# VectorE's order in the attention front written by hand, gate products in one bank, one unit of w_in per step

## The chip, the cores and the metric

The kernel runs on one core of a Trainium2 chip. The metric is the time of one execution in microseconds, as the median of several runs; less is better. The engines are TensorE (PE, with its weight loads PEld), VectorE (DVE), ScalarE (ACT), GpSimd (POOL) and SyncE (SP), which issues the DMAs. Each engine works through its own instructions in order and waits on semaphores for the others.

## What is computed

Three layers follow each other, all in float32 (the 18 blocks of 128 tokens are B x S = 2304 rows):

```
# 1 attention, 8 heads of 64, 576 positions, window of 128 back, ALiBi bias
scores = q @ k.T / 8 + slope * -(i - j)          where 0 <= i - j < 128, else -1e9
x = softmax(scores) @ v                          # -> [2304, 512]
# 2 dense layer
h = x @ w_in                                     # 512 -> 2048
g = max(0.01 * h, h)
y = g @ w_out                                    # 2048 -> 512
# 3 experts: 8 of them, 288 tokens each
logits = y @ w_gate                              # assigned greedily, highest logit first
out[mask_e] = relu(y[mask_e] @ w1[e]) @ w2[e]
```

The logits are not taken from y: the kernel multiplies w_out with w_gate first (below: the gate) and then uses g @ (w_out @ w_gate).

## The kernel before, in words

A matmul whose result has to be good to float32 is done as three passes of a faster type: each operand is split into a high part (`wh`, `xh`) and a low part (`wl`, `xl`, value minus high part). w_in and w_out arrive as 64-bit floats; 16 **units** of 128 x 1024 numbers (8 of w_in, 8 of w_out) have to be **converted** on the chip.

The front of the kernel, up to some 440 us of it, is one loop over **steps** s. One step handles one block of 64 queries of the attention, and beside it other work:

- `scores(j)`: 8 products into two PSUM banks of tag "s" (PE); `softmax_exp`: 4 fused add-and-minimum instructions on DVE (L437, into `neg` and `nm`) and 4 exponentials on ACT (L440, with the sums in `sm`); `softmax_norm`: DVE adds and inverts the sums (L447, L448) and scales two of four heads (L453), ACT the other two (L451).
- `transpose_p(j)`: probabilities transposed by PE into two banks of tag "t" and copied by ACT (`pts`, L465); `weighted(j)`: product with v into `xv` (tag "v", one bank); every second block it is split into `xh` (ACT, L490) and `xl` (DVE, L491).
- A unit k at the steps of `CONV_AT`: `conv_abs` (ACT, L345), `conv_high` (three DVE instructions, L356 to L358), `conv_low` (two on DVE, L365 and L366, and one addition on POOL, L368, into `dt`); for w_in also `in_high` (ACT, L350) and `in_low` (L372, on DVE for units 0 and 1, else on POOL). Units 8 to 15 (w_out) are stored to DRAM again.
- The **gate**: for each unit of w_out and each of its two halves h, `gate_transpose` (4 transposes, tag "t", ACT copy `wt`), one step later `gate_product` (4 products into `pg`, tag "l", which has one bank; DVE copy `gs`, L397), one step later `gate_fold` (1 product into `pw`, the same one bank; DVE copy to `wg`, L403).
- 72 **items** (c, fp), 2 (from step 14 on; before that up to 4) in each step as soon as their x and w_in are there: `expand` (24 matmuls into a bank of tag "h", which has two) and `expand_out`: `th` on ACT (L514), `gb` on DVE (L518), store to DRAM.
- From step 31 on the **late** logits: g of the first 6 chunks is loaded back (`gr`, L554) and multiplied with `wg`.

Behind the front follow, one after the other, the product with w_out (`po`, L223) with the assignment of tokens beside it, and the experts (L984, L1003).

What sets the order: for PE and ACT the order in the program text (`ENG_A`); for DVE, POOL and SP a list scheduler of the framework. A tile of a pool with n buffers is written again only when the work on its n-th predecessor is done; so with the one bank of tag "l" each `pg` and `pw` waits for DVE's copy of the one before.

Of the kernel before, what the change touches and what calls it, by code (L numbers as in the profile page):

```python
# [19 lines left out]
P = 128  # L20
# [50 lines left out]
NORM_A = (2, 3)  # L71
STAGES = 2
WINDOW = 128
# [53 lines left out]
def tile_attn_moe_moe2(ctx: ExitStack, tc: tile.TileContext, q_in, k_in, v, w_in, w_out, w_gate, w1, w2, consts, out):  # L127
# [18 lines left out]
    def C(name):  # L146
        return cst[:, COLS[name][0]:COLS[name][1]]
# [155 lines left out]
    with ExitStack() as actx:  # L303
# [70 lines left out]

        gate = {}

        def gate_transpose(k, h):
            w = conv[k]
            if h == 0:
                nc.sync.dma_start(wo_dram[k - 8], w)  # L380
            else:
                conv.pop(k)
            pt = bank("t", f"wtp_{k}_{h}").rearrange("p (d f) -> p d f", d=4)
            for d in range(4):
                T.transpose(pt[:, d, :], w[:, h * DM + d * P:h * DM + d * P + P], ident)  # L385
            wt = cv.tile([P, 4, P], F32, tag="wt", name=f"wt_{k}_{h}")
            A.activation(wt, pt, AF.Copy)
            gate[k, h] = wt

        def gate_product(k, h):  # L390
            wt = gate[k, h]
            pg = bank("l", f"pg_{k}_{h}", bufs=1)[:, :P]
            for d in range(4):
                T.matmul(pg[32 * d:32 * d + 32, :], gsb[:, d, :], wt[:, d, :], start=True,
                         stop=True, tile_position=(0, 32 * d))
            gs = cv.tile([P, P], F32, tag="gs", name=f"gs_{k}_{h}")
            V.tensor_copy(gs, pg)  # L397
            gate[k, h] = gs

        def gate_fold(k, h):  # L400
            pw = bank("l", f"pw_{k}_{h}", bufs=1)[:, :32]
            T.matmul(pw, gate.pop((k, h)), C("fold"), start=True, stop=True)
            V.tensor_copy(wg[:, 2 * (k - 8) + h, :], pw)  # L403


        st = {}
# [1 line left out]
        def scores(j):  # L408


            b, m = divmod(j, SQ)
            nk = keys_before(j)
            s = [bank("s", f"s_{j}_{a}")[:, :2 * nk].rearrange("p (h k) -> p h k", h=2) for a in range(2)]
            qt, t0 = qring[j // 3 % 2], j % 3 * Q
            for hf in range(2):
                for a in range(2):
                    for x in range(2):
                        c, rows = 2 * hf + x, slice(a * D, a * D + D)
                        T.matmul(s[a][x * Q:x * Q + Q, hf, :], qt[rows, c, t0:t0 + Q],  # L419
                                 ktile[b][rows, c, (m + 1) * Q - nk:(m + 1) * Q], start=True, stop=True,  # L420
                                 tile_position=(a * D, x * Q))
            st[j] = dict(nk=nk, s=s)

        def softmax_begin(j):
            d = st[j]
            d["neg"] = [apool.tile([P, 2, 3 * Q], F32, tag="neg", name=f"neg_{j}_{h}") for h in range(2)]
            d["nm"] = apool.tile([P, 4], F32, tag="nm", name=f"nm_{j}", bufs=2)
            d["sm"] = apool.tile([P, 4], F32, tag="sm", name=f"sm_{j}", bufs=2)
            d["pr"] = apool.tile([P, 4, 3 * Q], F32, tag="pr", name=f"pr_{j}", bufs=PRB)

        def softmax_exp(j, hf):
            d = st[j]
            nk = d["nk"]
            for a in range(2):
                i = 2 * hf + a
                neg = d["neg"][hf][:, a, :nk]
                V.tensor_tensor_reduce(  # L437
                    out=neg, in0=d["s"][a][:, hf, :], in1=bias_sb[:, i, 3 * Q - nk:],
                    scale=-0.125, scalar=3e38, op0=ALU.add, op1=ALU.min, accum_out=d["nm"][:, i:i + 1])
                A.activation(d["pr"][:, i, :nk], neg, AF.Exp, scale=-1.0, bias=d["nm"][:, i:i + 1],  # L440
                             accum_out=d["sm"][:, i:i + 1])

        def softmax_norm(j):
            d = st[j]
# [101 lines left out]

        late = {}

        def late_load(c, hf):
            assert not any(x[0] == c for x in items)  # L550
            for f4 in range(2 * hf, 2 * hf + 2):
# [5 lines left out]
        def late_logits(c, hf):  # L557
            for f4 in range(2 * hf, 2 * hf + 2):
                logits(c, f4, late.pop((c, f4)), "t")


# [4 lines left out]
        def at(s, f, *a):  # L566
            after.setdefault(s, []).append((f, *a))

        conv_at = {s: k for k, s in enumerate(CONV_AT)}
        for k, s in list(enumerate(CONV_AT))[8:]:  # L570
            for h in range(2):

                at(s + GLAG + h, gate_transpose, k, h)
                at(s + GLAG + h + 2, gate_fold, k, h)
                at(s + GLAG + h + 1, gate_product, k, h)
        gate_end = CONV_AT[15] + GLAG + 3
        late0 = gate_end + 2
        for c in range(LG0):
            for hf in range(2):
                at(late0 + 2 * c + hf - 1, late_load, c, hf)  # L580
                at(late0 + 2 * c + hf, late_logits, c, hf)
            at(late0 + 2 * c + 2, logits_fold, c)
        late_end = late0 + 2 * LG0

        if True:
# [19 lines left out]
            def prepare(j):  # L605

                if j and j % 3 == 0:
                    load_qk(j // 3 + 1)
# [19 lines left out]
            staged = []  # L628
            scores(0)
            prepare(0)  # L630
            while s <= max(NQ + 1, late_end) or items or pending or tail:

                now = [x for x in items if max(ready.get(x[0], 1 << 30), in_ready.get(x[1] | 1, 1 << 30)) <= s]
                now = now[:ITEMS_0 if s < ITEMS_S else 2]
# [1 line left out]
                    items.remove(x)  # L636
                k = conv_at.get(s)

                if s < NQ:
                    softmax_begin(s)  # L640
                    softmax_exp(s, 0)
                    softmax_exp(s, 1)
                    if s + 1 < NQ:
                        scores(s + 1)
                        prepare(s + 1)
                if 1 < s <= NQ + 1:
                    weighted(s - 2)
                    if (s - 2) % 4 == 3:
                        ready[(s - 2) // 4] = s + XLAG
                if 0 < s <= NQ:  # L650
                    transpose_p(s - 1)
                if s:
                    load_v(s + 1)
# [9 lines left out]
                for f in after.pop(s, ()):  # L663
                    f[0](*f[1:])
                for n, (c, fp) in enumerate(now):
                    expand(c, fp, 0)
                    expand(c, fp, 1)
# [6 lines left out]
                        convert_low(k)  # L674
                if not now:
                    convert_low(k)
                if s + 1 in conv_at:
                    conv_abs(conv_at[s + 1])
# [427 lines left out]
```

## Time and profile before

| | before |
|---|---|
| median of 3 runs | 944.03 us (942.78 to 944.92) |
| profiled execution: time / span | 939.93 us / 938.1 us |
| PE, PEld busy | 847.3 us (90%), 737.0 us (79%) |
| DVE, ACT, POOL busy | 525.8 us, 383.2 us, 109.0 us |
| chain that ended last: PE / DVE / ACT | 78% / 7% / 7% |
| mean granted TensorE clock | 0.970 |

The span goes from the first to the last instruction of the profiled execution. The busy time of PE is made of pipelined matmuls, so a busy PE is not a PE at its peak; what it can't hide are the stretches in which it waits, and those in which its granted clock is below 1. Where a line of the trace has a bracket, it gives the idle time of the engine ahead of it and what ended it.

### The profile page before, as it was taken

To read this page: it belongs to the slowest core of one execution; us is meant where nothing else is said; L and a number is where in the kernel's file an instruction comes from. 1 tells how busy PE (TensorE), PEld (TensorE's weight loads), DVE (VectorE), ACT (ScalarE), POOL (GpSimd) and SP (SyncE) were. 2 spreads that over 40 slices of the span, in tenths; PEclk is the share of its full clock that TensorE was granted. 3 is DMA by queue.
4 is the path that set the end of the run, shared out by engine and by line. 5 is a ranking of instruction groups with operands and counts; after the bars stand their busy time and mean duration, and the time that the engine had idled before them with its cause. 6 is when DMAs were issued, how large, how long until landed. Compare 5 with 4: busy or idle time off the path is not lost.

```text
span 938.1 us, 18698 instructions
## 1 busy us (share of the span) xinstructions
PE 847.3 (90%) x7590; PEld 737.0 (79%) x7590; DVE 525.8 (56%) x1339; ACT 383.2 (41%) x833; POOL 109.0 (12%) x104
## 2 busy tenths in 40 slices
PE   2787878788889989998999999998999999999996
PEld 2577767777778878787777767775889999999995
DVE  5876667536453443224877877877316545555550
ACT  3874635445445554223212131211215555555551
POOL 1323221112110000000000000000011221122211
PEclk9897989999899999999999999999999999999998
DMA  9774545646332796577342423222336555666640
GB/s 286 229 202 153 177 154 176 192 144 213 100 118 64 218 285 173 157 195 221 112 141 75 137 99 127 90 79 69 100 94 195 181 171 187 218 209 188 187 134 26
DMA packets 103637, 147.19 MB, mean 157 GB/s; under 512 B 6144, under 2 KB 74368, under 8 KB 101504
## 3 DMA queue, kind: packets, MB, share of 16 engines
q1 hardware_dynamic: 100480, 136.56, 47.4%
q0 software_dynamic: 3072, 9.44, 2.9%
q8 instruction: 60, 0.98, 0.4%
q14 instruction: 25, 0.20, 0.1%
HBM read 113.21 MB, written 32.77 MB: 156 GB/s over the span
## 4 chain that ended last, share of the span: by engine, by line
PE 78%; DVE 7%; ACT 7%; issue 5%; DMA 2%; POOL 1%; SPq 0%; POOLq 0%; ACTq 0%
PE po L223 23%; PE h L505 20%; PE m L984 10%; PE y L1003 10%; ACT pr L440 3%; PE cnt L804 3%; PE xv L480 2%; PE s L419 2%; PE pt L463 2%; PE lg L532 2%; DVE dt L358 1%; DVE neg L437 1%; PE wtp L385 1%; ACT dt L345 1%; ACT th L514 1%
## 5 line engine op out<-in xcount | busy, mean ns | idle before, releaser
L518 DVE TENSOR_TENSOR gb<-h,th 128x512 f32<-128x512 f32 x72 | 49.6, 690 | 159.4 <-ACT th L514 148.6
L223 PE MATMUL po<-wh_out,gol 128*128 128x512 f32 x272 | 112.0, 412 | 4.2 <-DVE gol L191 4.1
L223 PE MATMUL po<-wh_out,goh 128*128 128x512 f32 x272 | 110.6, 406 | 0.0
L223 PE MATMUL po<-wl_out,goh 128*128 128x512 f32 x272 | 110.4, 406 | 0.0
L514 ACT ACTIVATE th<-h 128x512 f32<-128x512 f32 x72 | 42.8, 596 | 157.0 <-PE h L505 157.0
L505 PE MATMUL h<-xh,wh_in 128*128 128x256 f32 x576 | 96.6, 292 | 7.7 <-DVE gb L518 7.7
L505 PE MATMUL h<-xh,wl_in 128*128 128x256 f32 x576 | 92.6, 284 | 0.0
L505 PE MATMUL h<-xl,wh_in 128*128 128x256 f32 x576 | 91.9, 283 | 0.0
L505 PEld LDWEIGHTS h<-xh,wh_in 128*128 128x128 f32 x576 | 80.5, 197 | 12.0 <-DVE gb L518 8.1
L160 DVE TENSOR_TENSOR wl_w<-st_w,wh_w 128x1024 fp32r<-128x1024 f32 x60 | 72.9, 1225 | 26.7 <-ACT wh_w L159 26.7
L183 ACT ACTIVATE goh<-gin 128x1024 fp32r<-128x1024 f32 x34 | 36.0, 1060 | 126.0 <-DMA gin<-g_dram 107.0
L505 PEld LDWEIGHTS h<-xh,wl_in 128*128 128x128 f32 x576 | 79.7, 195 | 0.2 <-POOL wl_in L372 0.2
L505 PEld LDWEIGHTS h<-xl,wh_in 128*128 128x128 f32 x576 | 79.4, 195 | 0.0
L1003 PE MATMUL y<-hh,wh_w 128*128 128x288 f32 x256 | 77.4, 302 | 0.0
L1003 PE MATMUL y<-hh,wl_w 128*128 128x288 f32 x256 | 75.6, 295 | 0.0
L1003 PE MATMUL y<-hl,wh_w 128*128 128x288 f32 x256 | 75.5, 295 | 0.0
L419 PE MATMUL s<-k,q 64*64 64x192 f32 (+2 forms) x576 | 36.3, 355 | 32.5 <-DVE nm L437 22.3
L159 ACT ACTIVATE wh_w<-st_w 128x1024 fp32r<-128x1024 f32 x60 | 62.4, 1053 | 2.8 <-DMA st_w<-in_w_dram 2.8
L223 PEld LDWEIGHTS po<-wh_out,gol 128*128 128x128 f32 x272 | 51.5, 189 | 15.1 <-DVE gol L191 5.4
L368 POOL TENSOR_TENSOR dt<-dt,de 128x1024 f32<-128x1024 f32 x16 | 38.3, 2392 | 206.7 <-DVE pr L453 79.1
L440 ACT ACTIVATE pr<-neg,nm 128x192 f32<-128x192 f32 (+2 forms) x144 | 60.8, 427 | 0.0
L223 PEld LDWEIGHTS po<-wl_out,goh 128*128 128x128 f32 x272 | 51.4, 189 | 10.2 <-issue 0.2
(220 smaller groups left out, 1607.7 us busy)
## 6 DMA issues: line engine op xcount, KB each, us to landing
st_w<-in_w_dram SPq DMA_DIRECT2D x64, 512.0 KB, 4.0
g_dram<-gb SPq DMA_DIRECT2D x72, 256.0 KB, 3.7
gin<-g_dram SPq DMA_DIRECT2D x34, 512.0 KB, 3.9
gr<-g_dram SPq DMA_DIRECT2D x48, 256.0 KB, 5.4
v<-in_v_dram SPq DMA_DIRECT2D x28, 384.0 KB, 4.7
raw<-in_w_in_dram SPq DMA_DIRECT2D x8, 1024.0 KB, 5.3
raw<-in_w_out_dram SPq DMA_DIRECT2D x8, 1024.0 KB, 5.1
x_dram<-xo SPq DMA_DIRECT2D x17, 256.0 KB, 2.0
```

The costliest lines, as they stand in the source:

```text
L159: A.activation(wh, st, AF.Copy)
L160: lo_engine.tensor_tensor(out=wl, in0=st, in1=wh.bitcast(F32), op=ALU.subtract)
L183: A.activation(wh, st, AF.Copy)
L223: T.matmul(po, g, w, start=(k == 0), stop=(k == 47))
L368: (V if k in ADD_V else GP).tensor_tensor(out=t, in0=t, in1=e, op=ALU.add)
L419: T.matmul(s[a][x * Q:x * Q + Q, hf, :], qt[rows, c, t0:t0 + Q], ktile[b][rows, c, (m + 1) * Q - nk:(m + 1) * Q], start=True, stop=True, t ...
L440: A.activation(d["pr"][:, i, :nk], neg, AF.Exp, scale=-1.0, bias=d["nm"][:, i:i + 1], accum_out=d["sm"][:, i:i + 1])
L505: T.matmul(hp[:, j, :], w[:, d, j * P:(j + 1) * P], x[:, d, :], start=(k == 0), stop=(k == 11))
L514: A.activation(th, hp, AF.Copy, scale=0.01)
L518: V.tensor_tensor(out=gbs[c][:, o:o + 2, :], in0=hp, in1=th, op=ALU.max)
L984: T.matmul(hp, w[:, d, :], x[:, d, :], start=(k == 0), stop=(k == 11))
L1003: T.matmul(yp, w, x[:, f, :], start=(k == 0), stop=(k == 23))
```

## The change

- DVE joins the engines whose order is that of the program text (`ENG_A`).
- The text is put in another order. Step s now handles `scores`, `softmax_exp` and `softmax_norm` of block s + 1, `transpose_p` of block s and `weighted` of block s - 1 (before: softmax of s, transposes of s - 1, weighted of s - 2). On DVE the softmax of a step stands ahead of the `gb` of its items.
- w_in is converted in steps 0 to 7, one unit each (before: steps 0 to 12); w_out in steps 9, 11, ... 23 (before: 13 to 25).
- The gate handles both halves of a unit together: one `pg` of 256 columns, one `gs` copy; `pw` moves to a bank of tag "t" and its copy to ACT. The transposes of a gate stand at the head of a step, ahead of the scores. 16 copies `gs` and 16 copies `wg` on DVE become 8 copies `gs` on DVE and 8 copies `wg` on ACT.
- Up to 4 items a step are taken until step 10 (before: 14); the late logits of a chunk come in one step in place of two, at its head.
- The second half of the heads is scored first.

```diff
-ENG_A = {ET.PE, ET.Activation}
+ENG_A = {ET.PE, ET.Activation, ET.DVE}
-CONV_AT = [0, 2, 4, 6, 8, 9, 11, 12, 13, 15, 16, 18, 20, 21, 23, 25]
+CONV_AT = [0, 1, 2, 3, 4, 5, 6, 7, 9, 11, 13, 15, 17, 19, 21, 23]
-ITEMS_0, ITEMS_S = 4, 14
+ITEMS_0, ITEMS_S = 4, 10
-GLAG = 1
+GLAG = 2
...
+        def gate_product(k):
+            wt = gate[k]
+            pg = bank("l", f"pg_{k}", bufs=1)[:, :2 * P].rearrange("p (h f) -> p h f", h=2)
...
+            gs = cv.tile([P, 2, P], F32, tag="gs", name=f"gs_{k}")
             V.tensor_copy(gs, pg)
...
+        def gate_fold(k):
+            pw = bank("t", f"pw_{k}")[:, :64].rearrange("p (h e) -> p h e", h=2)
...
+            A.activation(wg[:, 2 * (k - 8):2 * (k - 8) + 2, :], pw, AF.Copy)
...
-            for hf in range(2):
+            for hf in (1, 0):
...
+                for f in sorted(after.pop(s, ()), key=lambda f: f[0] is gate_transpose):
+                    f[0](*f[1:])
+                if s + 1 < NQ:
+                    scores(s + 1)
+                    prepare(s + 1)
+                    softmax_exp(s + 1)
+                if 0 < s <= NQ:
+                    weighted(s - 1)
+                    if (s - 1) % 4 == 3:
+                        ready[(s - 1) // 4] = s + XLAG
+                for k2 in products_of_gate:
+                    gate_product(k2)
...
+                    transpose_p(s)
+                load_v(s + 2)
                 if k is not None:
                     conv_high(k)
-                if s < NQ:
-                    softmax_norm(s)
+                if s + 1 < NQ:
+                    softmax_norm(s + 1)
```

**TensorE, a step with gate work.** In the program before (step 16), `pw` and `pg` stand one behind the other in the same bank, between the transposes of the probabilities and the items:

```order
L480 MATMUL xv_1841<-pts_0_1716,v_1397 64x64 x8
L480 MATMUL xv_1841<-pts_1_1723,v_1397 64x64 x8
L463 MATMUL pt_0_1858<-cst,pr_1672 96x128 x4
L463 MATMUL pt_1_1865<-cst,pr_1672 96x128 x4
L402 MATMUL pw_0_1884<-cst,gs_0_1742 128x32
L394 MATMUL pg_1_1887<-wt_1_1749,gsb 32x128 x4
L385 MATMUL wtp_0_1895<-cst,dt_1666 128x128 x4
L505 MATMUL h_4_1902<-xh_1116,wh_in_815 128x256 x4
```

In the changed program (head of step 15), fold and transposes stand ahead of the scores, and no `pg` behind a `pw`:

```order
L403 MATMUL pw_1851<-cst,gs_1765 128x32 x2
L384 MATMUL wtp_0_1857<-cst,dt_1559 128x128 x4
L384 MATMUL wtp_1_1863<-cst,dt_1559 128x128 x4
L421 MATMUL s_0_1869<-k_512,q_84 64x192 x2
L421 MATMUL s_1_1870<-k_512,q_84 64x192 x2
L421 MATMUL s_0_1869<-k_512,q_84 64x192 x2
L421 MATMUL s_1_1870<-k_512,q_84 64x192 x2
L480 MATMUL xv_1892<-pts_0_1772,v_1550 64x64 x8
L480 MATMUL xv_1892<-pts_1_1779,v_1550 64x64 x8
L463 MATMUL pt_0_1909<-cst,pr_1725 96x128 x4
```

The `pg` of both halves stands alone in the steps between, behind `xv`.

**VectorE, the same step 16 before.** The copy `wg` for which PE's `pg` waits stands behind the second pair of softmax instructions and two conversion instructions (`neg`, `nm`: softmax; `dt`, `de`: conversion; `rs`, `pr`: norm):

```order
L358 SCALAR_TENSOR_TENSOR dt_1816<-raw_1442,dt_1816 128x1024
L447 TENSOR_SCALAR rs_1877<-sm_1821 128x4
L437 ISA neg_1_1968,nm_1969<-s_0_1831,bias_sb 128x192
L437 ISA nm_1969 128x1
L437 ISA neg_1_1968,nm_1969<-s_1_1832,bias_sb 128x192
L437 ISA nm_1969 128x1
L403 COPY wg<-pw_0_1884 128x32
L365 TENSOR_SCALAR de_1931<-dt_1816 128x1024
L448 RECIPROCAL rs_1877<-rs_1877 128x4
L397 COPY gs_1_1892<-pg_1_1887 128x128
L366 SCALAR_TENSOR_TENSOR de_1931<-raw_1442,de_1931 128x1024
```

In the changed program (step 14) only the copy `gs` is left on DVE, and no unit is converted in its step:

```order
L436 ISA neg_1_1731,nm_1723<-s_1_1711,bias_sb 128x192
L436 ISA nm_1723 128x1
L491 TENSOR_TENSOR xl_1753<-xv_1602,xh_1752 128x4x128
L396 COPY gs_1765<-pg_1756 128x256
L447 TENSOR_SCALAR rs_1783<-sm_1724 128x4
L448 RECIPROCAL rs_1783<-rs_1783 128x4
L453 TENSOR_SCALAR pr_1725<-pr_1725,rs_1783 128x192 x2
L518 TENSOR_TENSOR gb_2_1819<-h_2_1792,th_2_1817 128x512
L518 TENSOR_TENSOR gb_2_1819<-h_3_1821,th_3_1846 128x512
```

The two `gb` stand behind the whole softmax of the next block.

**VectorE, the conversion of w_in.** Between units 3 and 4 of the changed program (steps 3 and 4) stand the four softmax instructions and `xl`, then the next unit begins:

```order
L366 SCALAR_TENSOR_TENSOR de_416<-raw_268,de_416 128x1024
L436 ISA neg_0_436,nm_433<-s_0_423,bias_sb 128x192
L436 ISA nm_433 128x1
L436 ISA neg_0_436,nm_433<-s_1_424,bias_sb 128x192
L436 ISA nm_433 128x1
L436 ISA neg_1_441,nm_433<-s_0_423,bias_sb 128x192
L436 ISA nm_433 128x1
L436 ISA neg_1_441,nm_433<-s_1_424,bias_sb 128x192
L436 ISA nm_433 128x1
L491 TENSOR_TENSOR xl_304<-xv_368,xh_303 128x4x128
L356 TENSOR_SCALAR dt_411<-dt_411 128x1024
L357 TENSOR_SCALAR dt_411<-dt_411 128x1024
```

In the program before the same units stand in steps 6 and 8, with a step of softmax and items between them.

## Rows read from the trace of the kernel before

**Rows 1.** Windows: start:end, length, busy us (count) by engine, granted clock, DMA.

```profile
137.00:312.20 175.20, 148.47 (x1739) 135.71 (x1738) 90.24 (x283) 86.41 (x240) 17.05 (x7) 0.94 0.46 145
312.20:440.20 128.00, 119.12 (x1333) 101.87 (x1332) 48.20 (x131) 51.91 (x126) 0.52 (x1) 1.00 0.75 213
440.20:938.00 497.80, 483.81 (x3491) 413.73 (x3489) 290.60 (x679) 170.53 (x261) 52.89 (x72) 0.99 0.42 134
```

**Rows 2.** PE's waits from 137 to 312.2 us: total us, times, longest.

```profile
PE pg L394 <- DVE wg L403: 20.7, 13, 2.6
PE pg L394 <- DVE gs L397: 2.5, 2, 1.7
PE pw L402 <- DVE wg L403: 2.0, 2, 1.1
PE wtp L385 <- ACT pts L465: 1.5, 2, 1.2
```

**Rows 3.** PE's waits from 12.5 to 137 us.

```profile
PE s L419 <- DVE nm L437: 21.7, 7, 5.4
PE h L505 <- DVE gb L518: 7.7, 2, 5.9
```

**Rows 4.** Timeline of PE: start us, us, line, tile, count, [idle before].

```profile
101.46 0.74 PE L505 MATMUL h<-xh,wh_in 128*128 128x256 f32 x4 [1.74 <-DVE gb L518]
...
128.96 1.23 PE L505 MATMUL h<-xh,wh_in 128*128 128x256 f32 x4 [5.92 <-DVE gb L518]
...
137.00 0.88 PE L419 MATMUL s<-k,q 64*64 64x192 f32 x16
...
140.31 0.63 PE L385 MATMUL wtp<-cst,dt 128*128 128x128 f32 x4 [0.34 <-ACT pts L465]
140.70 0.71 PE L505 MATMUL h<-xh,wh_in 128*128 128x256 f32 x4
...
146.32 0.88 PE L419 MATMUL s<-k,q 64*64 64x192 f32 x16
...
162.56 0.43 PE L394 MATMUL pg<-wt,gsb 128*32 128x128 f32 x8 [2.57 <-DVE wg L403]
...
319.78 0.88 PE L419 MATMUL s<-k,q 64*64 64x192 f32 x16
```

**Rows 5.** Timeline of DVE and POOL: units 7 and 8 converted one behind the other.

```profile
109.63 0.69 DVE L357 TENSOR_SCALAR dt<-dt 128x1024 int32<-128x1024 int32 x1
...
114.42 0.54 DVE L453 TENSOR_SCALAR pr<-pr,rs 128x192 f32<-128x192 f32 x2
...
115.25 2.37 POOL L368 TENSOR_TENSOR dt<-dt,de 128x1024 f32<-128x1024 f32 x1 [8.80 <-ACT wh_in L350]
...
116.24 1.93 DVE L356 TENSOR_SCALAR dt<-dt 128x1024 f32<-128x1024 f32 x1 [1.28 <-ACT dt L345]
...
117.70 2.74 POOL L372 TENSOR_TENSOR wl_in<-dt,wh_in 128x1024 fp32r<-128x1024 f32 x1
...
118.21 2.78 DVE L357 TENSOR_SCALAR dt<-dt 128x1024 int32<-128x1024 int32 x1
...
123.22 0.68 DVE L491 TENSOR_TENSOR xl<-xv,xh 128x512 fp32r<-128x512 f32 x1
...
124.54 1.23 DVE L366 SCALAR_TENSOR_TENSOR de<-raw,de 128x1024 f32<-128x1024 uint32 x1
...
125.68 2.63 DVE L453 TENSOR_SCALAR pr<-pr,rs 128x192 f32<-128x192 f32 x2
```

**Rows 6.** Timeline of ACT: the first unit's start, and `th` after a wait.

```profile
11.37 1.12 ACT L345 ACTIVATE dt<-raw 128x1024 f32<-128x1024 f32 x1 [9.13 <-DMA raw<-in_w_in_dram]
...
134.37 0.60 ACT L514 ACTIVATE th<-h 128x512 f32<-128x512 f32 x1 [7.92 <-PE h L505]
```

**Rows 7.** Groups by form, 12.5 to 137 us: count, busy us, mean ns, idle before.

```profile
L440 ACT ACTIVATE pr<-neg,nm 128x192 f32<-128x192 f32 x40 | 17.6, 447 | 0.0
...
L437 DVE CUSTOM_DVE_ANT_0 neg<-s,bias_sb 128x192 f32<-128x192 f32 x44 | 13.8, 351 | 2.7 <-ACT pr L440 2.5 <-PE pt L463 0.2
```

More of the change, by code (lines that the diff above doesn't have):

```diff
@@ L375, in tile_attn_moe_moe2 @@
         gate = {}
[L377 to L396, printed above, removed]
-            V.tensor_copy(gs, pg)
[L398 to L403, printed above, removed]
+        def gate_transpose(k):
+            w = conv.pop(k)
+            nc.sync.dma_start(wo_dram[k - 8], w)
+            wt = cv.tile([P, 2, 4, P], F32, tag="wt", name=f"wt_{k}")
+            for h in range(2):
+                pt = bank("t", f"wtp_{k}_{h}").rearrange("p (d f) -> p d f", d=4)
+                for d in range(4):
+                    T.transpose(pt[:, d, :], w[:, h * DM + d * P:h * DM + d * P + P], ident)
+                A.activation(wt[:, h], pt, AF.Copy)
+            gate[k] = wt
@@ new lines, in gate_product @@
+        def gate_product(k):
+            wt = gate[k]
+            pg = bank("l", f"pg_{k}", bufs=1)[:, :2 * P].rearrange("p (h f) -> p h f", h=2)
+            for h in range(2):
+                for d in range(4):
+                    T.matmul(pg[32 * d:32 * d + 32, h, :], gsb[:, d, :], wt[:, h, d, :], start=True,
+                             stop=True, tile_position=(0, 32 * d))
+            gs = cv.tile([P, 2, P], F32, tag="gs", name=f"gs_{k}")
+            V.tensor_copy(gs, pg)
+            gate[k] = gs
@@ L406, in tile_attn_moe_moe2 @@
+        def gate_fold(k):
+            pw = bank("t", f"pw_{k}")[:, :64].rearrange("p (h e) -> p h e", h=2)
+            gs = gate.pop(k)
+            for h in range(2):
+                T.matmul(pw[:, h, :], gs[:, h, :], C("fold"), start=True, stop=True)
+            A.activation(wg[:, 2 * (k - 8):2 * (k - 8) + 2, :], pw, AF.Copy)
         st = {}
@@ L422, in scores, with softmax_exp @@
             st[j] = dict(nk=nk, s=s)
[L424 to L431, printed above, removed]
+        def softmax_exp(j):
             d = st[j]
             nk = d["nk"]
[L434 to L441, printed above, removed]
+            nm = apool.tile([P, 4], F32, tag="nm", name=f"nm_{j}", bufs=2)
+            sm = apool.tile([P, 4], F32, tag="sm", name=f"sm_{j}", bufs=2)
+            pr = apool.tile([P, 4, 3 * Q], F32, tag="pr", name=f"pr_{j}", bufs=PRB)
+            for hf in range(2):
+                neg = apool.tile([P, 2, 3 * Q], F32, tag="neg", name=f"neg_{j}_{hf}")
+                for a in range(2):
+                    i = 2 * hf + a
+                    V.tensor_tensor_reduce(
+                        out=neg[:, a, :nk], in0=d["s"][a][:, hf, :], in1=bias_sb[:, i, 3 * Q - nk:],
+                        scale=-0.125, scalar=3e38, op0=ALU.add, op1=ALU.min, accum_out=nm[:, i:i + 1])
+                    A.activation(pr[:, i, :nk], neg[:, a, :nk], AF.Exp, scale=-1.0, bias=nm[:, i:i + 1],
+                                 accum_out=sm[:, i:i + 1])
+            d.update(sm=sm, pr=pr)
         def softmax_norm(j):
@@ L547, in tile_attn_moe_moe2, with late_load @@
         late = {}
-        def late_load(c, hf):
+        def late_load(c):
             assert not any(x[0] == c for x in items)
-            for f4 in range(2 * hf, 2 * hf + 2):
+            for f4 in range(4):
                 t = late_pool.tile([P, 4, 256], F32, tag="gr", name=f"gr_{c}_{f4}", bufs=LATEB)
@@ L555, in late_load, with late_logits @@
                 late[c, f4] = t
-        def late_logits(c, hf):
-            for f4 in range(2 * hf, 2 * hf + 2):
+        def late_logits(c):
+            for f4 in range(4):
                 logits(c, f4, late.pop((c, f4)), "t")
@@ L569, in tile_attn_moe_moe2 @@
         conv_at = {s: k for k, s in enumerate(CONV_AT)}
+        products_of_gate, loads_late = [], []
         for k, s in list(enumerate(CONV_AT))[8:]:
[L571 to L576, printed above, removed]
+            at(s + GLAG + 2, gate_fold, k)
+            at(s + GLAG, gate_transpose, k)
+            at(s + GLAG + 1, products_of_gate.append, k)
+        gate_end = CONV_AT[15] + GLAG + 2
         late0 = gate_end + 2
         for c in range(LG0):
[L579 to L582, printed above, removed]
+            at(late0 + 2 * c - 1, loads_late.append, c)
+            at(late0 + 2 * c, late_logits, c)
+            at(late0 + 2 * c + 1, logits_fold, c)
         late_end = late0 + 2 * LG0
@@ L662, in tile_attn_moe_moe2 @@
                     f[0](*f[1:])
-                for f in after.pop(s, ()):
-                    f[0](*f[1:])
+                for c in loads_late:
+                    late_load(c)
+                loads_late.clear()
+                if s + 1 in conv_at:
+                    conv_abs(conv_at[s + 1])
                 for n, (c, fp) in enumerate(now):
```

21 lines of the change are left out of this document (4 added, 17 removed).

## The prediction

> **What bounds the kernel now.** First the stages. Behind 440.2 us PE is busy 483.8 of 497.8 us at a clock of 0.99 [rows 1]: that part can only move as a block, earlier or later. From 137.0 to 312.2 us PE is busy 148.5 of 175.2 us and its mean granted clock is 0.94; from 312.2 to 440.2 us it is busy 119.1 of 128.0 at a clock of 1.00. So the front has time to give, most of it in the stage with the gate. Second, what PE waits for there: `pg` for the copies `wg` and `gs`, 20.7 and 2.5 us, `pw` for `wg` 2.0, `wtp` for `pts` 1.5, together 26.7 us [rows 2], which is all of the 26.7 us in which PE is idle in that stage. The reader is to see that no large engine load is behind it: a product into the only bank of tag "l" waits for a copy that stands in VectorE's row behind softmax and conversion, up to 2.57 us each time [rows 4]. Third, ahead of 137 us: PE waits 21.7 us for `nm` and 7.7 us for `gb`, both of VectorE [rows 3]. There VectorE, with softmax and the conversion, is the bound, and GpSimd behind it.
>
> I compare at one point: the start of the step that takes items (2,0) and (2,1). Behind it both programs have 56 items, two a step, in 28 steps. It is step 14 before, at 137.0 us [rows 4], and step 13 after.
>
> **Gate copies (the gain).** A step before of 9.32 us, from 137.00 to 146.32 us, holds scores, `xv`, `pt`, two items, a wait of 0.34 and one set of transposes of 0.4 [rows 4]; without the last two it is 8.6 us. Fifteen of them are 129 us; the steps with fewer keys save some 3; the gate's own products are an estimated 15 (8 units of 1.85: 0.4 for each half's transposes, as from 140.31 to 140.70, 0.4 for each half's `pg`, some 0.15 for each fold). That is 141 us of work for a stage of 175.2: 34 us too many. 26.7 of them are the waits; the other 7 I put down to the slower clock (0.94 is a mixture of the two levels 2.4 and 1.2 GHz; 6% of 175 us would be 10.5, so 7 is not too much). After the change each `pg` follows the last one by two steps, its copy `gs` does not sit behind a conversion, and `pw` has a bank of tag "t". What is late next: at the head of a gate step the second set of transposes takes the bank of `pw`, and so waits for ScalarE's copy, which stands behind the last `th` of the step before (0.60 us [rows 6]): I take 0.5 us of PE for each of 8 units, 4 us. Gain: 26.7 + 7 - 4 = **30 us**. Bounds: 21 if the clock gives nothing back and every unit waits 0.7 us (26.7 - 5.6), 34 if no wait is left.
>
> Does VectorE keep up in these steps? With a unit it has four softmax instructions (1.1 us, 4 x 0.28: 351 ns less the overlap of 0.07 [rows 7]), conversion (2.35 + 1.75), norm 0.8, two `gb` of 0.6 each: 7.2 us against some 10 of PE; without a unit 4. It waits for the second `th` until 0.6 us behind PE's last item, and takes the next scores 0.5 us late; that is hidden by the items. GpSimd's one addition of 2.37 us [rows 5] then runs beside softmax. Yes, with some 2 us to spare.
>
> **One unit of w_in per step (the cost).** The one place before where a unit directly follows another: from 114.42 us, the end of unit 7 on VectorE, to 125.68, the end of unit 8 [rows 5]: 11.26 us. 1.28 of that is a wait for `dt` of ScalarE, 0.61 `xl`; without them 9.37. It shows why it is long: a fast scalar instruction of VectorE (L356, L357) that meets a GpSimd instruction ends only after it: 1.93 and 2.78 us where a free one takes 0.69. Softmax instructions and `gb` are not held. The changed program puts the four softmax instructions there, 1.1 us of the 2.37 of GpSimd's first instruction, and then meets both: 2.4 + 0.6 + 2.8 + 1.14 + norm 0.8 + 1.75 = 9.5. I take 9.4. The walk, as estimates from the same rows:
> - Unit 0: `dt` is there at 12.4 [rows 6] (the DMA is issued as before). Four exponentials 1.3, norm 0.7, softmax of block 1 0.9, 2.35, norm 0.6, 1.75, GpSimd 2.4, `in_low` on VectorE 1.15, for which VectorE now stands still: 23.6. Unit 1: 1.1 + 2.35 + 0.8 + 1.75 + 2.4 + 1.2: 33.2.
> - Unit 2: `xl` waits for `xh`, which on ScalarE stands behind four exponentials of 447 ns [rows 7]: 1.65 more, and 0.6; 41.4. Units 3 and 4, 9.4 each: 60.2.
> - Unit 5 comes with four items. `gb` of the first stands ahead of `conv_low`, and its `th` on ScalarE behind norm and `conv_abs`: 2.5 more, end of `conv_low` 72.1. The third item waits for that `gb`, 70.6, and after the wait PE is slow: an item after a wait of 5.92 us took 5.4 us (128.96 to 134.37 [rows 4, 6]), against 2.75 else. PE ends at 78.7, VectorE at 79.9.
> - Unit 6 with `xl` and two items: 90.6. Unit 7: 100.0; GpSimd's two instructions behind it end at 104.8, and the last item of chunk 0 needs them: step 8 ends at 107.5.
> - Steps 9 (2.9 + 4 x 2.75), 10, 11 (8.5 each, one set of gate transposes 0.85) and 12 (3.7, no items): step 13 starts at **143 us**, 6 later than 137.0. PE has one block of scores more behind it, 0.8.
>
> Bounds of the cost: five units (3 to 7) at the full 11.26 us add 9.5; if they cost VectorE nothing for GpSimd (7.1 each) they take 11.5 less.
>
> **Other edits.** The stage from 312.2 to 440.2 us keeps its work; its 8.9 us of idle time can change by some 3 either way, as the late logits stand elsewhere in the step. Their loads need as many bytes as before; the four buffers are free from the head of a step, and used two steps later. 16 copies fewer on VectorE and 8 more on ScalarE are beside other work: ScalarE is busy 86.4 of 175.2 us [rows 1]. The order of the halves of the heads is worth nothing that a row shows.
>
> **Sum.** 30 - 6 - 0.8 = 23 us off the profiled execution: 939.9 to 917 us. The median before, 944.0, lies 4.1 above that execution; I take the same difference off it: **921 us**.
>
> **The rivals.**
> - *The units cost their full 11.26 us*: 9.5 more, 930 us. For it: that is the only place of its kind, and unit 5 waits besides; against it: half of what I took off was a wait for ScalarE that the new order doesn't have.
> - *GpSimd waits, not VectorE.* In the rows GpSimd's L372 was there 0.5 us ahead of L357 and VectorE lost; L372 itself took 2.74 against 2.37, since it came upon L356. With two fast instructions in a row, VectorE can hold GpSimd off each time; units take 7.1 us: 11.5 off, 910 us. The Trainium skill (SBUF — State Buffer, Who interferes with whom) states the rule for it: the shared port pair is an exclusive lock, held for the whole instruction, and the one that issues first blocks the other. By the order of issue in the new program GpSimd is first, as in the rows, for `conv_low` ends before softmax; so I give this little.
> - *The wait passes to ScalarE.* If the fold's copy there comes as late as VectorE's did (2.57 us [rows 4]), 8 units wait 20 us in place of 4, with some 4 of slow clock: gain 3 us, 941 us. Against it: ahead of that copy stands one `th`, not a softmax.
> - *Slower: the two banks of the items.* On VectorE `gb` now stands behind the norm of the next block, which waits for its exponentials. If that holds the first item's bank past the next step's start, PE waits in each of the 16 steps from 13 to 28. The shorter of the waits of that kind took 1.74 us [rows 4]: 28 us, 949 us; it turns the sign from 1.4 us a step (23 / 16). Against it: by the count above the first `gb` ends 3 us ahead of need.
>
> **How the numbers follow.** My forecast, 912 to 928, has 0.57; full price of the units 0.18 (926 to 936); GpSimd waits 0.09 (906 to 914); wait passes to ScalarE 0.06; slower 0.10. The range, 909 to 936, leaves out the last two and half of the third. A measurement of this kernel can tell some 0.2%, 1.9 us, from no change. Faster: 0.57 + 0.18 + 0.09 and a third of the ScalarE case, 0.86; the rest of that case is the same, 0.04; slower 0.10.
>
> **What would show it.** Right: no wait of `pg` for `wg`, a granted clock of 0.98 or more from step 13 on, steps of 9 to 10 us in the gate stage; `dt` of units 3 to 7 some 9.4 us apart on VectorE with L356 and L357 at two to three times 0.69 us; items (2,0) at about 143 us and the last items' end near 417 us. Wrong: PE waits for `gb` in each step from 13 on, units 11 us apart, or `pw` and the second transposes each waiting over 1 us for ScalarE.

## The result and the profile after

The changed kernel takes 918.75 us (median of 4 runs, 917.14 to 919.14); the kernel before took 943.40 us beside it (4 runs, 941.42 to 944.92). The ratio is 0.9737, 95% interval 0.9714 to 0.9759. The forecast was 921.0, with 909 to 936.

The profiled execution has a span of 915.2 us. First the page's busy times and VectorE's `gb`, then the windows, cut where expansions (2,0), expansions (6,0) and the work behind the last expansion begin (columns as in [rows 1]):

```profile
span 915.2 us, 18665 instructions
PE 841.4 (92%) x7590; PEld 734.6 (80%) x7590; DVE 521.9 (57%) x1315; ACT 387.0 (42%) x841; POOL 108.9 (12%) x104
L518 DVE TENSOR_TENSOR gb<-h,th 128x512 f32<-128x512 f32 x72 | 49.7, 691 | 109.1 <-ACT th L514 108.5
```

```profile
12.50:159.20 146.70, 102.76 (x1075) 91.61 (x1076) 102.59 (x246) 79.31 (x220) 39.16 (x17) 0.93 0.61 182
159.20:303.60 144.40, 144.40 (x1806) 134.03 (x1805) 84.99 (x268) 88.89 (x252) 14.23 (x6) 1.00 0.63 187
303.60:417.30 113.70, 108.52 (x1211) 94.25 (x1210) 42.99 (x118) 45.82 (x108) 0.52 (x1) 0.97 0.78 206
417.30:915.00 497.70, 483.69 (x3472) 413.26 (x3471) 289.90 (x677) 170.36 (x261) 52.86 (x72) 0.99 0.42 134
```

The kernel before, cut at the same three places of its program:

```profile
12.50:140.70 128.20, 96.88 (x1061) 86.75 (x1061) 97.85 (x249) 75.19 (x215) 36.46 (x16) 0.89 0.63 194
140.70:322.00 181.30, 154.91 (x1806) 142.08 (x1804) 93.00 (x292) 89.73 (x252) 17.05 (x7) 0.94 0.48 147
322.00:440.20 118.20, 109.33 (x1208) 92.72 (x1207) 42.93 (x112) 45.12 (x104) 0.52 (x1) 1.00 0.76 216
```

So the early part costs 18.5 us, the gate stage gives 36.9, the late stage gives 4.5 more, and what stands behind the last expansion is the same (497.8 in [rows 1], 497.7 now). In the gate stage PE is busy 144.40 of 144.40 us: the waits of [rows 2] are gone, and the clock is 1.00.

The matmul counts of the gate stage, 1806 in both, are equal by chance. After the change the stage holds 35 matmuls of the gate less (188 against 223, as the first unit is done ahead of (2,0)) and 32 of the late logits more, which take 1.9 us. What is the same in both are the 768 matmuls of the expansions. One of their three groups, before and then after (busy us, mean ns of one, idle before):

```profile
L505 PE MATMUL h<-xh,wh_in 128*128 128x256 f32 x256 | 43.4, 294 | 0.0
...
L505 PE MATMUL h<-xh,wh_in 128*128 128x256 f32 x256 | 41.3, 283 | 0.0
```

The three together take 126.1 us before, at a mean clock of 0.94, and 120.8 after, at 1.00.

PE's waits from 12.5 to 159.2 us after, and from 303.6 to 417.3 (columns as in [rows 2] and [rows 3]):

```profile
PE pt L463 <- DVE pr L453: 15.4, 7, 3.5
PE s L421 <- DVE nm L436: 9.2, 2, 8.2
...
PE pw L403 <- DVE rs L447: 2.0, 1, 2.0
PE wtp L384 <- ACT wg L404: 1.1, 1, 1.1
...
PE pt L463 <- DVE lt L545: 4.6, 1, 4.6
```

Two things are new. VectorE stands still in the first two units. The timeline of after (start, us, engine, line, out<-in, in brackets the idle time before and its releaser):

```profile
23.63 1.23 DVE L372 TENSOR_TENSOR wl_in<-dt,wh_in 128x1024 fp32r<-128x1024 f32 x1 [2.85 <-POOL dt L368]
...
32.75 1.12 ACT L345 ACTIVATE dt<-raw 128x1024 f32<-128x1024 f32 x1 [3.01 <-DMA raw<-in_w_in_dram]
33.77 1.05 ACT L350 ACTIVATE wh_in<-dt 128x1024 fp32r<-128x1024 f32 x1
34.89 2.34 POOL L368 TENSOR_TENSOR dt<-dt,de 128x1024 f32<-128x1024 f32 x1 [11.30 <-ACT wh_in L350]
...
37.26 1.23 DVE L372 TENSOR_TENSOR wl_in<-dt,wh_in 128x1024 fp32r<-128x1024 f32 x1 [5.97 <-POOL dt L368]
...
41.78 0.68 DVE L356 TENSOR_SCALAR dt<-dt 128x1024 f32<-128x1024 f32 x1
```

Read it downwards: `raw` of unit 2, asked for at 20.95 us, lands at 32.7. ScalarE's abs of unit 2 (L345) waits for it, and `in_high` of unit 1 (L350) stands behind that abs (the changed program puts `conv_abs` of the next unit ahead of the expansions and of `in_high`, a move that the list of the change leaves out); GpSimd's sum of unit 1 needs `in_high`, and VectorE's `in_low` of unit 1 needs the sum. All softmax behind it waits too.

The other is a stop of PE behind the transposes of 311.55 us, in the same timeline (SPq is SyncE's queue; the last row is PE's own timeline):

```profile
302.74 4.55 SPq L554 DMA_DIRECT2D gr<-g_dram  x2
...
307.39 0.73 SPq L169 DMA_DIRECT2D st_out<-wo_dram  x1
...
314.25 1.06 ACT L159 ACTIVATE wh_out<-st_out 128x1024 fp32r<-128x1024 f32 x1 [3.29 <-DMA st_out<-wo_dram]
315.34 1.22 DVE L160 TENSOR_TENSOR wl_out<-st_out,wh_out 128x1024 fp32r<-128x1024 f32 x1 [3.12 <-ACT wh_out L159]
316.48 0.17 DVE L545 COPY lt<-pl 128x16 f32<-128x16 f32 x1
...
316.79 1.06 PE L463 MATMUL pt<-cst,pr 128*96 128x128 f32 x4 [4.60 <-DVE lt L545]
```

The copy `lt` takes 0.17 us and frees a bank that `pt` needs, but stands in VectorE's fixed row behind the split of a tail weight, whose transfer was issued only at 307.39, behind loads of `gr`. Behind the stop the granted clock is 0.5 (1.2 GHz) for 6.8 us.

### The profile page after: what moved, and what is told of

Read it like the earlier page. It is cut to its first block, busy times and chain, and to the rows that moved or that the text cites. A ratio compares the mean times of both kernels' runs of the same rounds, so it can differ in the third digit from the quotient of the medians.

```text
span 915.2 us, 18665 instructions
## 1 busy us (share of the span) xinstructions
PE 841.4 (92%) x7590; PEld 734.6 (80%) x7590; DVE 521.9 (57%) x1315; ACT 387.0 (42%) x841; POOL 108.9 (12%) x104
## 4 chain that ended last, share of the span: by engine, by line
PE 79%; DVE 9%; ACT 3%; issue 3%; DMA 3%; POOL 2%; SPq 0%; POOLq 0%; ACTq 0%; DVEq 0%
PE po L223 22%; PE h L505 20%; PE m L986 10%; PE y L1005 10%; PE xv L480 3%; PE cnt L806 3%; PE pt L463 2%; DMA raw<-in_w_in_dram 2%; PE lg L532 2%; PE s L421 2%; DVE dt L357 1%; DVE dt L356 1%; DVE dt L358 1%; PE wtp L384 1%; ACT pr L439 1%
## 5 line engine op out<-in xcount | busy, mean ns | idle before, releaser
L223 PE MATMUL po<-wh_out,gol 128*128 128x512 f32 x272 | 112.5, 414 | 4.7 <-DVE gol L191 4.6
L368 POOL TENSOR_TENSOR dt<-dt,de 128x1024 f32<-128x1024 f32 x16 | 37.9, 2366 | 187.3 <-DVE de L366 115.6
```

What stands on the lines that cost most here:

```text
L223: T.matmul(po, g, w, start=(k == 0), stop=(k == 47))
L368: (V if k in ADD_V else GP).tensor_tensor(out=t, in0=t, in1=e, op=ALU.add)
```

## The experiments

"Stage" below is the time from expansions (2,0) to (6,0), "late" from (6,0) to the last expansion's end, both to within 0.2 us. In us, from each kernel's trace; the time is the median of its runs, the ratio is to runs of the kernel before on the same chip:

| kernel | time | ratio, 95% | (0,0) | (2,0) | stage | late |
|---|---|---|---|---|---|---|
| before | 943.40 | | 47.7 | 140.7 | 181.3 | 118.2 |
| after | 918.75 | 0.9737 (0.9714 to 0.9759) | 67.5 | 159.2 | 144.4 | 113.7 |
| e1_w_in_spread | 913.01 | 0.9707 (0.9678 to 0.9736) | 53.7 | 155.6 | 147.7 | 106.9 |
| e7_scheduled | 900.04 | 0.9560 (0.9538 to 0.9582) | 61.4 | 148.5 | 144.4 | 106.1 |
| e4_abs_behind | 915.73 | 0.9717 (0.9694 to 0.9739) | 63.9 | 153.0 | 149.9 | 113.2 |
| e5_in_low_pool | 914.23 | 0.9706 (0.9689 to 0.9723) | 65.0 | 155.9 | 144.4 | 113.6 |
| e2_gate_only | 928.07 | 0.9856 (0.9831 to 0.9882) | 47.3 | 140.1 | 165.8 | 120.6 |
| e3_fold_as_before | 911.28 | 0.9692 (0.9660 to 0.9723) | 67.8 | 156.6 | 143.1 | 112.1 |
| e8_old_gate | 947.12 | 1.0052 (1.0022 to 1.0081) | 65.3 | 157.4 | 170.5 | 112.5 |
| e8b_old_gate_lag2 | 908.19 | 0.9651 (0.9608 to 0.9694) | 65.8 | 153.0 | 142.6 | 110.2 |
| e6_one_split | 908.30 | 0.9643 (0.9627 to 0.9660) | 65.8 | 156.7 | 144.4 | 107.0 |
| e9_sched_spread | 893.88 | 0.9496 (0.9455 to 0.9538) | 45.2 | 143.0 | 144.7 | 105.6 |
| e11_sched_in_low_v | 894.88 | 0.9499 (0.9458 to 0.9540) | 61.6 | 147.2 | 144.7 | 105.9 |
| e12_sched_spread_in_low_v | 887.66 | 0.9432 (0.9405 to 0.9460) | 45.4 | 136.9 | 144.8 | 105.5 |

How far one execution can be trusted: e6 and after are the same program until behind the gate stage, and their (2,0) differ by 2.5 us (156.7 and 159.2). After, e3, e6, e8 and e8b have the same text up to step 9; their VectorE starts unit 2 at 41.8, 42.1, 40.0, 39.5 and 40.1 us, as the transfer for it lands between 30.5 and 33.0. So a difference of some 2.5 us in a single trace ahead of (2,0) says nothing about an edit.

### The early part: packing, or VectorE's order?

**e1**: packing undone.

```diff
-CONV_AT = [0, 1, 2, 3, 4, 5, 6, 7, 9, 11, 13, 15, 17, 19, 21, 23]
+CONV_AT = [0, 2, 4, 6, 8, 9, 11, 12, 13, 15, 16, 18, 20, 21, 23, 25]
...
-ITEMS_0, ITEMS_S = 4, 10
+ITEMS_0, ITEMS_S = 4, 14
```

> The changed kernel with one part undone: the sixteen units of conversion stand at the steps of the kernel before (w_in at steps 0, 2, 4, 6, 8, 9, 11, 12, w_out from 13 to 25) and four expansions a step are allowed up to step 14 again. Theory: the packing of w_in is a cost, because expansions (2,0) began at 159.2 us after and at 140.7 us before. With it undone (2,0) should begin near 141 to 147 us, the 258 us of TensorE from there to the last expansion stay as they are, and the time is 900 to 908 us. Rival: the packing earns its place, since w_out and with it the late logits end two steps sooner; then the end is set by the steps and not by TensorE, and this kernel takes 918 to 930 us, with TensorE waiting behind step 25.

Both fell. The first expansion comes 13.8 us sooner, but (2,0) only 3.7, far from 141 to 147 and little more than two executions of one program differ by. The late stage is 6.8 us shorter, as only 1.4 us of the stop are left there; the gate stage is 3.3 us longer. So with the order by hand packing is not the main thing that makes the early part dear.

**e7**: only the order by hand undone.

```diff
-ENG_A = {ET.PE, ET.Activation, ET.DVE}
+ENG_A = {ET.PE, ET.Activation}
```

> The changed kernel with VectorE's order left to the scheduler again, all else as changed. Theory that the banks carry the gain: the gate stage keeps TensorE without waits, the time is 912 to 925 us, and the stop of TensorE at step 30 (4.6 us, for a copy of the logits behind a split that waited for its transfer) can go. Rival, that the order carries it: waits of s for nm or of pt for pr come back in 160 to 304 us, 10 to 25 us with the clock, and the time is 930 to 945 us.

This is faster than either theory: 16.7 us less than after, by ratio. The stage is 144.4 us in both, so with the gate's new text the order by hand carries none of the gain there; it costs 10.7 us ahead of (2,0) and 7.6 behind (6,0), by these two traces. The stage in e7:

```profile
148.40:292.80 144.40, 144.40 (x1807) 134.03 (x1805) 87.62 (x271) 90.32 (x259) 14.43 (x6) 1.00 0.63 189
```

From the timeline of e7, VectorE's first instructions of units 2 and 3, and GpSimd's second one of unit 2:

```profile
30.18 0.69 DVE L356 TENSOR_SCALAR dt<-dt 128x1024 f32<-128x1024 f32 x1
...
30.90 2.73 DVE L357 TENSOR_SCALAR dt<-dt 128x1024 int32<-128x1024 int32 x1
...
39.98 0.69 DVE L356 TENSOR_SCALAR dt<-dt 128x1024 f32<-128x1024 f32 x1
40.70 2.73 DVE L357 TENSOR_SCALAR dt<-dt 128x1024 int32<-128x1024 int32 x1
...
42.96 2.69 POOL L372 TENSOR_TENSOR wl_in<-dt,wh_in 128x1024 fp32r<-128x1024 f32 x1
43.47 3.26 DVE L358 SCALAR_TENSOR_TENSOR dt<-raw,dt 128x1024 int32<-128x1024 int32 x1
```

Unit 2 starts at 30.18 us, 11.6 us ahead of the 41.78 above; unit 7 ends at 98.0 on VectorE, against 109.3, so the lead lasts, and (2,0) still has 10.7 of it. Some 4.3 us of it come with the transfer, which e7 asks for at 18.2 us and has by 28.4; the rest is VectorE not standing behind unit 1. The period from unit to unit (9.8 us here) is no shorter than forecast.

**e4** and **e5** each take away one reason for VectorE to stand still.

```diff
# e4: behind the expansions, not ahead of them
-                if s + 1 in conv_at:
-                    conv_abs(conv_at[s + 1])
                 for n, (c, fp) in enumerate(now):
...
                 if not now:
                     convert_low(k)
+                if s + 1 in conv_at:
+                    conv_abs(conv_at[s + 1])
# e5
-IN_V = (0, 1)
+IN_V = ()
```

> The changed kernel with one move undone: the conversion's first instruction of the next unit (abs on ScalarE) stands behind the expansions and the end of the unit at hand again, not ahead of them. After the change in_high of unit 1 stood behind abs of unit 2, which waited for a transfer until 32.75 us, and VectorE, in order, stood 5.97 us in front of in_low of unit 1. Theory: an in-order VectorE standing still in units 0 and 1 makes the early part dear. Then here unit 1 ends about 4 us sooner, expansions (2,0) begin near 155 us instead of 159.2, and the time is 913 to 916 us. Rival: the transfer of unit 2 binds, and unit 2 starts as late as before: 918 to 921 us.

> The changed kernel with the low halves of units 0 and 1 subtracted on GpSimd, as those of units 2 to 7 are, and not on VectorE. VectorE then has nothing in the first two units that waits for GpSimd (2.85 and 5.97 us after the change). Theory of the standing VectorE: unit 2's first instruction on VectorE goes from 41.8 to 34 to 37 us (with VectorE's order left to the scheduler it was 30.2), (2,0) begins at 152 to 155 us, and the time is 910 to 915 us. Rival: GpSimd's four long operations in two units slow VectorE's by as much as the waits were: 917 to 922 us.

Both times lie in the range of the first theory, but that doesn't establish it. Unit 2 starts at 38.97 us in e4 and 37.44 in e5, 2.8 and 4.3 sooner than after, and (2,0) comes at 153.0 and 155.9; against the 39.5 to 42.1 of the unchanged text the lead of e4 is not clear of chance, and that of e5 is 2.1 us. By ratio the time falls by some 2 and 3 us, and the intervals overlap with that of after, so as gains they are not established. e4 also pays in the stage, where the abs now stands ahead of the fold's copy on ScalarE. PE's waits from 153 to 302.9 us in e4:

```profile
PE wtp L384 <- ACT wg L404: 4.9, 5, 1.0
```

Neither mend alone gets back the 11.6 us that the scheduler's order has.

**e9, e11, e12**: the free order with packing undone, with `in_low` on VectorE, and with both.

```diff
# e9: e7 and e1 together; e11: e7 and the lines below; e12: all three
-IN_V = (0, 1)
+IN_V = tuple(range(8))
```

> The changed kernel with VectorE's order left to the scheduler and w_in spread over the steps of before. Theory that packing and order by hand cost apart: with VectorE free to go on, (2,0) comes at 141 to 145 us (148.5 with the packing, 140.7 before) and the time is 890 to 897 us. Rival: by the scheduler's order VectorE is what fills the first 148 us (112.5 of 135.9 us busy), the work ahead of (2,0) is the same wherever it stands, and the time is 898 to 904 us.

> The changed kernel with VectorE's order left to the scheduler and all eight low halves of w_in subtracted on VectorE, not only the first two. GpSimd's subtraction takes 2.7 us, during which one VectorE instruction takes 3.2 us instead of 1.2; on VectorE it takes 1.2 us. Theory of the slowed neighbour: VectorE gains 0.8 us at each of six units and a unit ends sooner, (2,0) begins at 142 to 146 us and the time is 893 to 898 us. Rival: VectorE is the bound of that stretch and just gets 1.2 us more at each of six units: (2,0) at 152 to 157 us, 903 to 909 us.

> The two last together: VectorE's order left to the scheduler, w_in spread over the steps of before, all eight low halves of w_in on VectorE. Theory that the two gains are of two kinds (a later place for work that nobody awaits, and less work held up by GpSimd) and add up: 900.0 less 6.2 less 5.2, so 887 to 891 us. Rival, that both buy the same slack of VectorE ahead of expansions (2,0), so that the second brings nothing or its 1.2 us at six units: 893 to 898 us.

The first theory holds in all three times. With the free order, undoing the packing brings 5.5 us at (2,0); by hand it had brought 3.7. In e11 (2,0) came at 147.2, a little later than expected: its profiled execution took 896.94 us, the highest of its runs (894.08 to 896.94), so its trace does not place all of the 5 us. e12 takes 887.66 us, ratio 0.9432, and beats both kernels: (2,0) at 136.9 us, 22.3 ahead of the changed kernel. GpSimd's busy time ahead of (2,0) is 22.41 us there, against 39.16 after:

```profile
12.50:136.90 124.40, 97.70 (x1095) 86.73 (x1096) 96.40 (x255) 78.09 (x221) 22.41 (x10) 0.88 0.68 202
```

### The gate stage: which edit carries the 36.9 us?

**e2**: the new gate functions alone in the kernel before; **e3**: the changed kernel with bank and engine of the fold as before.

```diff
# e2, in the kernel before, with the three gate functions of the changed kernel
...
+            at(s + GLAG, gate_transpose, k)
+            at(s + GLAG + 2, gate_fold, k)
+            at(s + GLAG + 1, gate_product, k)
# e3, in the changed kernel
-            pw = bank("t", f"pw_{k}")[:, :64].rearrange("p (h e) -> p h e", h=2)
+            pw = bank("l", f"pw_{k}", bufs=1)[:, :64].rearrange("p (h e) -> p h e", h=2)
...
-            A.activation(wg[:, 2 * (k - 8):2 * (k - 8) + 2, :], pw, AF.Copy)
+            V.tensor_copy(wg[:, 2 * (k - 8):2 * (k - 8) + 2, :], pw)
```

> The kernel before with the gate's new text alone: both halves in one step, the fold's product in bank t, its copy on ScalarE; VectorE's order is still the scheduler's and w_in is spread as before. Theory: the waits of the products for the copies (26.7 us in 137 to 312 us) were a matter of one bank shared by products and folds, so this alone brings 20 to 35 us: 908 to 924 us, with no more than 5 us of waits of pg and pw in that stretch. Rival: they were a matter of VectorE's order (the copies lay behind expansions' outputs and conversions in its queue), so that without the order by hand the product waits for its bank's copy all the same: 932 to 946 us.

> The changed kernel with the fold's product back in bank l, of which there is one, and its copy back on VectorE. Theory that the bank carries the gain of the gate stage: pg waits for the copy of wg again, 1 to 2.5 us at each of eight units, some of the clock is lost too, and the time is 930 to 940 us. Rival, that VectorE's order by hand carries it: the copy stands at the head of its step ahead of all that is long, fold and product lie a stretch of scores and weighted sums apart, and the time is 917 to 922 us with at most 3 us of such waits.

e2 lies between its two theories: the stage goes to 165.8 us, 15.5 of the 36.9. The waits of `pg` are gone, but `pw` and the transposes now wait for ScalarE. Its PE waits from 140 to 312 us:

```profile
PE pw L403 <- ACT pts L466: 7.1, 8, 2.0
PE wtp L384 <- ACT wg L404: 5.5, 2, 2.9
```

In e3 the theory of the bank fell, and the time, 911.28 us, lies below the rival's 917 to 922 too: the stage is 143.1 us without a wait, though product and fold share the one bank again:

```profile
156.50:299.60 143.10, 143.10 (x1806) 133.95 (x1805) 86.90 (x277) 88.11 (x249) 14.25 (x6) 1.00 0.65 193
```

**e8** and **e8b**: all of the gate's text as before in the changed loop, with lag 1 and lag 2 (e8b differs by this line alone).

```diff
# the three gate functions as in the kernel before
...
-            at(s + GLAG + 2, gate_fold, k)
-            at(s + GLAG, gate_transpose, k)
-            at(s + GLAG + 1, products_of_gate.append, k)
+            for h in range(2):
+                at(s + GLAG + h + 2, gate_fold, k, h)
+                at(s + GLAG + h, gate_transpose, k, h)
+                at(s + GLAG + h + 1, products_of_gate.append, (k, h))
# e8 only
-GLAG = 2
+GLAG = 1
```

> The changed kernel with the gate's text of before in the changed loop: two halves in two steps, product and fold both in bank l, both copies on VectorE. The complement of the run that put the gate's new text into the kernel before, where the stretch from (2,0) to (6,0) went from 181.3 to 165.8 us. Theory that the two parts add up (gate text 15.5 us, the loop's order 21.4 us): that stretch takes 157 to 162 us here, and the time is 930 to 936 us. Rival, that the loop's order alone keeps TensorE without waits, whatever the banks: 144 to 149 us and 914 to 923 us.

> The run with the gate's text of before in the changed loop, with the one number put right that confounded it: the transposes come two steps behind their unit's conversion, as in the changed kernel, and not one. In that run TensorE waited 22.6 us, all for GpSimd's sum of the unit (7 waits of the transposes), and 1.3 us for copies. Theory: what frees TensorE in the gate stage is where the copies and products stand in a step, with a lag of two, whatever the banks and halves; then (2,0) to (6,0) takes 144 to 149 us and the time is 914 to 922 us. Rival: two halves in two steps make each product wait for the copy in its bank, 1 us at 14 places and some clock: 155 to 162 us there and 928 to 936 us.

Both theories missed in e8 (stage 170.5 us). It was confounded by its lag, as its waits from 157.4 to 327.9 us show: with the transposes at the head of a step, a lag of one step puts them ahead of GpSimd's sum of the same unit.

```profile
PE wtp L385 <- POOL dt L368: 19.4, 6, 3.7
```

(Its median of 947.12 is over ten runs from 937.07 to 949.77; the profiled one took 939.43.) With the lag put right, e8b lies below both ranges of its theory (908.19 us; 142.6 for the stage), with PE busy throughout at full clock, at 16 single halves with both copies on VectorE and one bank:

```profile
153.00:295.60 142.60, 142.60 (x1780) 132.78 (x1779) 87.12 (x290) 88.11 (x249) 14.25 (x6) 1.00 0.60 181
```

The window of after holds the late logits of one chunk (1.9 us), which here fall behind it; without them the two are equally long. So with the order by hand neither banks nor halves nor the fold's engine are needed. More than that: e8b is faster than the changed kernel, with intervals that don't overlap (0.9651 against 0.9737, some 8 us), so the gate's new text brought nothing in the changed loop. 3.5 of the 8 us stand in the late stage, where the stop is 1.4 us instead of 4.6; no run traces the rest to the gate's text. e3 points the same way, but its interval touches that of after.

What stays is the place in the step (fold and transposes at its head, the product behind `xv`, softmax ahead of the expansions' outputs) with a lag of two. With the scheduler's order too the changed loop brings the greater part: the stage is 165.8 us in e2 and 144.4 in e7, 21.4 less, and 144.7 in e9, where the conversion stands as before. These edits were not taken apart further; bank and copies of before were not tried with the scheduler's order in the changed loop, nor a lag of two in the loop of before.

### The late stage

**e6**: one split of a tail weight in a step until seven are left.

```diff
-                for _ in range(2):
+                for _ in range(1 if len(tail) > 7 else 2):
```

> The changed kernel with one split of a tail weight in a step instead of two until seven are left. Theory of the late stage: TensorE's stop at step 30 (4.60 us for a copy of the logits, and half the clock for 6.8 us behind it) came from VectorE standing in a split whose transfer had been issued 7 us before; with one a step the transfer is a step old, the stretch from expansions (6,0) to the last goes from 113.7 to 106 us (106.1 was measured with the scheduler's order), and the time is 909 to 912 us. Rival: the later splits only move the wait behind the last expansion, where the first product needs them: 917 to 922 us.

The theory holds: late goes from 113.7 to 107.0 us, 0.5 us is left of the stop, and the clock is 1.00 there. The time, 908.30 us, is 0.7 below the range of the theory. In e7 the stop does not occur, and in e1 1.4 us of it are left (late 106.1 and 106.9).

```profile
301.10:408.00 106.90, 105.80 (x1211) 91.90 (x1209) 43.75 (x115) 46.13 (x107) 0.53 (x1) 1.00 0.82 219
```

## Why the prediction was right, and which of its steps were not

The total came out 2.3 us off with some luck: at the cut that the prediction chose (the start of step 14 before, of step 13 after) the part ahead cost 15.2 us, forecast 6, and what stands behind it gave 38.1, forecast 29.2. The misses of 9.2 and 8.9 us cancel. So of the signs that were named, the last items' end near 417 us came (417.3), and items (2,0) at about 143 did not (159.2).

- **The gate stage** (forecast +30; measured +36.9 from (2,0) to (6,0), +33.6 from the prediction's cut, 185.0 to 151.4). The waits, 26.7, were right in size and went fully. The slow clock was put at 7 us. PE's busy time from (2,0) to (6,0) fell by 154.91 - 144.40 = 10.5; 5.3 of that stands in the expansions, the same matmuls at the two mean clocks; the rest is in the main the gate's own work, which is not the same in both windows, so 7 is not refuted. The 4 us of new waits for ScalarE did not come in the stage. The one foreseen, of the second transposes for the fold's copy, came once, at the head of step 13 (1.14 us, beside 1.96 of the fold for VectorE); in e4, where ScalarE is later, such waits are 4.9 us. Of the reasons named, the bank is not what the gain rests on once the order is by hand (e3, e8b); with the scheduler's order and in the loop of before the gate's new text, bank included, gave 15.5 us (e2). The place of the copies in the step and the lag of two stand.
- **The early walk** (forecast -6, step 13 at 143 us; measured 152.2, items (2,0) at 159.2). The units' price was close in sum: units 3 to 7 took 62.2 us in all, from 47.1 to 109.3, forecast 58.6. L356 and L357 are both held as in [rows 5] in units 3, 5 and 7; in unit 4 only L356 is, as `xl`, which the walk left out there, fills the time, and in unit 6 neither. At the start of unit 5, in the timeline of after:

```profile
68.97 2.44 DVE L356 TENSOR_SCALAR dt<-dt 128x1024 f32<-128x1024 f32 x1
...
71.44 2.78 DVE L357 TENSOR_SCALAR dt<-dt 128x1024 int32<-128x1024 int32 x1
```

  The step that failed is unit 1: it was costed by VectorE's and GpSimd's durations alone, 33.2 us, and ended at 38.4 (1.2 us of the 5.2 were there at the end of unit 0). `raw` of unit 2 was taken as landed, though the trace of before has 9.0 us for the same transfer, and the move of `conv_abs` ahead of `in_high` was not followed along ScalarE's row. Of the 9.2 us at step 13, 5.2 come from there, some 4 from the other units. Step 13 itself took 7.0 us to its first item, where the forecast comes to 4.5 (3.7 in the trace of before and 0.8): the waits of 1.96 and 1.14 us fall at its head.
- **The late stage** (±3, measured +4.5; PE's idle time there fell from 8.9 to 5.2 us) hid two things: 6.7 us more were to be had, and the order by hand gave them back in one stop (e6). The text did not look at where the tail's splits stand in VectorE's row.
- **Rivals.** GpSimd did not wait in VectorE's place: its L368 took 2.34 to 2.39 us in units 0 to 7 of after. The two banks of the expansions cost nothing in the stage, and ScalarE's copies cost nothing there either. The full price of the units would have made units 3 to 7 68.1 us (58.6 and 9.5); 62.2 is nearer to the forecast.
- **What the forecast never asked** was what the order by hand itself is worth. By e7 it is a loss of some 17 us; the sum took it as free and the gain as one parcel.

## What to carry to other kernels

An order by hand on an engine turns each late input into a stop for all that stands behind it; follow every instruction that is put in a row to its last input, transfers and other engines' rows included, above all in the first steps. Undo an order by hand alone and measure it before crediting it: here 21.4 of the gate stage's 36.9 us (e2 against e7) came with where the work stands in the program's steps, and the scheduler made some 17 us more of the same text. When PE waits at full load, count the slow clock behind the waits as well, by the busy time of the same instructions at either clock, and make sure that they are the same: equal counts in two windows are not proof.

## What the runs showed of the hardware that was not expected

- Not only VectorE's instructions with one input are held by GpSimd. L358, with two inputs in SBUF, took 3.26 us in e7, where it met GpSimd's L372 (42.96 us, 2.69 long), against 1.2 free. Groups of lines of VectorE from 12.5 to 145 us, after and then e7 (mean ns of one behind the busy time):

```profile
L358 DVE SCALAR_TENSOR_TENSOR dt<-raw,dt 128x1024 int32<-128x1024 int32 x10 | 12.2, 1225 | 0.3
...
L358 DVE SCALAR_TENSOR_TENSOR dt<-raw,dt 128x1024 int32<-128x1024 int32 x10 | 20.4, 2043 | 0.3
```

  The Trainium skill (SBUF — State Buffer, Who interferes with whom) says that an instruction of VectorE with two SBUF inputs contends with a GpSimd instruction that reads SBUF; the trace of e7 agrees.
- It goes the other way round where VectorE is first. In e7, L368 of GpSimd began 0.02 us behind L358 and took 3.44 us, against 2.34 to 2.39 in units 0 to 7 of the changed kernel:

```profile
72.14 1.23 DVE L358 SCALAR_TENSOR_TENSOR dt<-raw,dt 128x1024 int32<-128x1024 int32 x1
...
72.16 3.44 POOL L368 TENSOR_TENSOR dt<-dt,de 128x1024 f32<-128x1024 f32 x1 [5.39 <-DVE dt L357]
```

- The transfer of 1 MB for unit 2 took 11.8 us to land (20.95 to 32.7), against a median of 5.4 for the eight of its kind in the same trace. It is no single event: the same transfer took 9.0 us before, 10.0 in e6 and 11.3 in e3.
- SyncE's queue took 4.55 us to issue two loads of `gr`, and a transfer that VectorE needed stood behind them (rows of 302.74 and 307.39 us above).
